# One transpose per score step, PV in fours, and the FFN 22 steps behind, in a fused attention and FFN kernel

## The chip, the cores and the metric

The kernel runs on one core of a Trainium2 chip. The metric is the device time of one execution in microseconds (us), the median of several runs. Engines are named as the profile names them: PE is the matrix engine (PEld its weight loads), DVE the vector engine, ACT the scalar engine, POOL the GpSimd engine, SP the engine whose queue issues most of the DMAs.

## The reference

Four batches of eight heads, 768 positions, head size 64. Queries and keys are each assigned to one of 16 clusters, and a query sees only the keys of its own cluster. The heads' outputs, side by side, are the 512 wide input of a gated FFN with 1536 hidden columns.

```python
q_assign = argmax(einsum('bhsd,hcd->bhsc', q_n, c_n), -1)   # k_assign the same way
mask = q_assign[:, :, :, None] == k_assign[:, :, None, :]
attn = softmax(where(mask, q @ k.T / sqrt(D), -1e9))
x = (attn @ v).transpose(0, 2, 1, 3).reshape(B * S, H * D)   # 3072 x 512
xn = x / sqrt(mean(x * x) + 1e-6) * rms_g
out = (silu(xn @ w_gate) * (xn @ w_val)) @ w_out             # 3072 x 512, float32
```

## The kernel before

The order of all instructions is written out by hand; each engine takes its own in that order, and a tile's next writer waits for its last readers.

**Steps and slots.** A *slot* is one head of one batch: 32 slots. The scores of a slot, keys on partitions, are 6 x 768 = 4608 columns, cut into nine *steps* of 512: 288 steps. In a step the loop calls `score_chunk`, then one piece of the FFN (`ffn_next`), then `flush(1)` (which lets all but the newest pending DVE operation go), then the product with v of the slot before (PV), then `extras`, the side work entered for that step with `at`.

**Scores.** Up to step `FFN0` two steps are taken together: up to four matmuls (L280) fill a 1024 column tile `scw` of which there are two, and one ACT exponential (L283) writes `pT`. A slot is so four wide chunks and a short one. From `FFN0` on each step has its own 512 column tile `sc`. The mask is 16 extra rows of `aug`: one-hot rows of the clusters, so the matmul has 80 rows.

**PV.** 36 matmuls of 65 columns a slot (L294), six a step in steps 2 to 7 of the next slot, into one accumulator `acc`; at its step 8 DVE takes the reciprocal of the sums and writes `x` (L303, L304).

**Preparation of a pair of heads** (`prep_parts`): twelve float32 transposes of q and k on PE in four groups of three (L183, T0 to T3), each group copied to `qk32` by DVE or ACT (L187, L189); casts to `aug` on POOL (L206); four cluster matmuls into `sp` (L222); on DVE the arg max (`tr`, `mx`, `oh`, `ohT`); four small DMAs on SP that place the one-hot rows in `aug`; the cast of v on POOL (L211). The tiles `tp` and `sp` share two buffers. Pair `pi` of 16 is used from step 18 `pi` on, and its parts lie at fixed steps after `base`, which is 18 (`pi` - 2) plus a small offset for pairs 2, 3 and 6.

**FFN.** A batch is two halves of 384 tokens, twelve blocks each of 128 hidden columns, and a block has three pieces: `gp` (four matmuls with the gate weights, ACT tanh `th`, then DVE `uu`), `vp` (four matmuls, then DVE `gvT`), and `dp` (three matmuls with the output weights, for the half before). `gp` and `vp` share two buffers (`gv`): a `gp` needs that the `uu` of the block before has read its buffer, a `vp` the `gvT` of the block before. After four `dp` pieces the sum goes through `ob` (DVE, or ACT in the tail) to the output; `dp` has one buffer. One piece is issued a step from `FFN0` = 72 + `LAG` on, with `LAG` = 24.

**Between them**, `rms_parts`: at step 8 of a batch's following slot its `x` is whole; in the steps after it the sums of squares `jk` (ACT, DVE), the power -0.5 on POOL (`ir`), three `xn` on DVE (L336), and one transposing DMA from SP to `xnT`, which the FFN reads; then the same for the second half. These lie at steps 9 to 26 after the batch's 72 steps.

**The tail** after step 287 issues what is left of the FFN. PSUM has eight banks: `ps_d` 1, `ps_pv` 1, `ps_t` 2, and four for `ps_wide`, given to `sc` and `gv` at `FFN0`.

Of the kernel before, what the change touches and what calls it, by code (L numbers as in the profile page):

```python
# [8 lines left out]
F32 = mybir.dt.float32  # L9
# [10 lines left out]
def kernel(  # L20
# [40 lines left out]
    ffn = ctx.enter_context(tc.tile_pool(name="ffn", bufs=2))  # L61
    ps_d = ctx.enter_context(tc.tile_pool(name="ps_d", bufs=1, space=PSUM))
    ps_pv = ctx.enter_context(tc.tile_pool(name="ps_pv", bufs=1, space=PSUM))
    ps_t = ctx.enter_context(tc.tile_pool(name="ps_t", bufs=2, space=PSUM))

    wide = ExitStack()
    ps_wide = wide.enter_context(tc.tile_pool(name="ps_wide", bufs=2, space=PSUM))
    late = {}
    LAG = 24
    FFN0 = H * NCH + LAG  # L70

# [48 lines left out]
    def keep_warm(n):  # L120
        w_ps = ps_d.tile([P, 512], F32, name="w_ps", tag="d")
        for _ in range(n):
            nc.tensor.matmul(w_ps, lhsT=zeros[:, 0:P], rhs=zeros, start=True, stop=True)
# [44 lines left out]
    def prep_parts(pi):  # L168
# [3 lines left out]

        def t_group(g):
            a, side = divmod(g, 2)
            if g == 0:
                qk32[0] = prep.tile([P, 4, HS], F32, name="qk32", tag="qk32")
            if pi == 0 and g >= 2:
                tp = ps_wide.tile([P, 2 * CH], F32, name="tpw", tag="scw")[:, 0:HS]
            else:
                tp = ps_t.tile([P, HS], F32, name="tp", tag="t")  # L180
            src = loads[pi][side]
            for i in range(TH):
                nc.tensor.transpose(tp[:, i * P:(i + 1) * P], src[:, a, i * P:(i + 1) * P], ident_f)  # L183
            dst = qk32[0][:, g, :]
            on_dve = (g % 2 == 0 if pi == 0 else g > 1 if pi == 1 else pi < 6 or g % 2)
            if on_dve:
                nc.vector.tensor_copy(dst, tp)  # L187
            else:
                nc.scalar.copy(dst, tp)  # L189
            state[g] = tp  # L190

# [21 lines left out]

        def assign():
            h0 = 2 * (pi % NP)
            if pi == 0:
                sp = ps_d.tile([P, CH], F32, name="spd", tag="d")[:, 0:HS]
            else:
                sp = ps_t.tile([P, HS], F32, name="sp", tag="t")
            for j in range(4):  # L220
                side, a = divmod(j, 2)
                nc.tensor.matmul(sp[32 * j:32 * j + 32, :], lhsT=cbd[:, h0 + a, :, :].rearrange("p c r -> p (c r)"),  # L222
                                 rhs=qk32[0][:, 2 * a + side, :], start=True, stop=True,
                                 tile_position=(0, 32 * j))
            state["sp"] = sp

# [28 lines left out]

        return [lambda: t_group(0), lambda: t_group(1), lambda: t_group(2), lambda: t_group(3), casts, assign, argmax1, argmax2, place, casts_v]

# [28 lines left out]

    def pv_group(slot, g):
        pi, a = divmod(slot, 2)
        vb = vbf[pi % NSET]
        if g == 0:  # L290
            accs[slot] = ps_pv.tile([P, ST, D + 1], F32, name="acc", tag="acc")
        acc = accs[slot]
        for kc in range(ST):
            nc.tensor.matmul(acc[:, TORD[g], :], lhsT=pts[slot][:, kc * S + g * P:kc * S + (g + 1) * P],  # L294
                             rhs=vb[:, a, TORD[kc], :], start=(kc == 0), stop=(kc == ST - 1))

    def pv_norm(slot):
# [55 lines left out]

    def ffn_piece(n, kind, tail):
        half = n // FC
# [26 lines left out]
        elif kind == 2 and half >= 1:  # L382
            hf = half - 1
            b, m = divmod(hf, 2)
            t = m * TH + fc // 4
            qd = fc % 4
            if qd == 0:
                pool, tag = (ps_pv, "acc") if tail and (fc // 4) % 2 else (ps_d, "d")
                cur["d"] = pool.tile([P, DM], F32, name="dp", tag=tag)
            dp = cur["d"]  # L390
            for i in range(3):
                f = qd * 3 + i
                tl = fc // 4
                nc.tensor.matmul(dp, lhsT=gvT[hf][:, f, tl * P:(tl + 1) * P], rhs=wo[:, f, :],  # L394
                                 start=(f == 0), stop=(f == FC - 1))
            if qd == 3:
                def after():
                    ob = ffn.tile([P, DM], F32, name="ob", tag="ob", bufs=3)
                    if tail:
                        nc.scalar.activation(ob, dp, ACT.Copy, scale=0.5)  # L400
                    else:
                        nc.vector.tensor_scalar_mul(ob, dp, 0.5)  # L402
                    nc.sync.dma_start(out=out_v[b, :, t, :], in_=ob)
                pend.append(after)
# [7 lines left out]

    def ffn_next(limit, tail=False):
        n, kind = divmod(fpos[0], 3)
        if n >= limit:
            return False
        fpos[0] += 1
        ffn_piece(n, kind, tail)
        return True
# [8 lines left out]

    T0, T1, T2, T3, CAST, SP, ARG1, ARG2, PLACE, CASTV = range(10)
    p0, p1 = prep_parts(0), prep_parts(1)  # L430
    keep_warm(6)
    for i in (T0, T1, T2, T3):
        p0[i]()
# [5 lines left out]
    p0[ARG1]()  # L439
    p1[T0]()  # L440
    p0[ARG2]()
    p0[PLACE]()
    for i in (T1, T2, T3, CAST):
        p1[i]()
    keep_warm(8)
    for i in (SP, ARG1, ARG2, PLACE, CASTV):
        p1[i]()
    load_pair(3)
    at(4, lambda: load_pair(4))
    at(30, lambda: nc.sync.dma_start(out=g_b, in_=moe_rms_g.unsqueeze(0).to_broadcast([P, DM])))  # L450
    for pi in range(2, B * NP):
        base = 2 * NCH * (pi - 2) + {2: 4, 3: 1, 6: 6}.get(pi, 0)
        for fn, step in zip(prep_parts(pi), (0, 1, 3, 4, 5, 8, 9, 11, 11, 9)):
            at(base + step, fn)
        if pi < B * NP - 3:
            at({6: 100, 7: 106}.get(pi, base + 11), lambda pi=pi: load_pair(pi + 3))
    for i, step in enumerate((50, 58, 68, 76, 86, 94, 100, 105, 111, 117, 123, 129)):
# [10 lines left out]
    for step in range(NT):  # L468
        slot, j = divmod(step, NCH)
        if step == FFN0:  # L470
            wide.close()
            for nm in ("sc", "gv"):
                late[nm] = ctx.enter_context(tc.tile_pool(name="ps_" + nm, bufs=2, space=PSUM))
        score_chunk(slot, j)
        ffn_next(min(B, max(0, (step - LAG) // (H * NCH))) * 2 * FC)
        flush(1)
        if slot > 0 and 2 <= j < 2 + ST:
            pv_group(slot - 1, j - 2)
        if slot > 0 and j == 2 + ST:
            pv_norm(slot - 1)  # L480
        extras(step)

    for j in range(28):
# [4 lines left out]
        flush(1)  # L488
        if 2 <= j < 2 + ST:
            pv_group(NS - 1, j - 2)  # L490
        if j == 2 + ST:
            pv_norm(NS - 1)
        extras(NT + j)
# [32 lines left out]
```

## Time and profile before

| | |
|---|---|
| median of 3 runs | 366.11 us (364.82 to 366.2) |
| the profiled execution | 365.05 us, its span 363.2 us |
| mean granted PE clock | 0.989 |
| PE busy | 335.2 us, 92% of the span |
| ACT / DVE / POOL busy | 229.4 / 223.5 / 86.3 us |
| PE's share of the chain that ended last | 72% (DVE 14%, ACT 7%) |
| first exponential of the scores, first FFN matmul, last exponential (start) | 15.9, 76.0, 282.8 us |

The profile is of one execution, 1.06 us below the median, and 1.8 us of its time lie outside the span. Its 40 slices are 9.08 us each. So the kernel has four stages: until 15.9 us the first loads and the preparation of two pairs; then ten slots of scores and PV alone, until the FFN begins at 76.0 us; then scores, PV and FFN together until 283 us; then the tail.

### The profile page before, as it was taken

What the parts mean: (1) busy time and instruction counts of PE and PEld (TensorE: products, weight loads), DVE (VectorE), ACT (ScalarE), POOL (GpSimd) and SP (SyncE); (2) the same over time, 40 slices, a digit from 0 to 9 for tenths busy, and PEclk for the clock granted to TensorE, in tenths of its full rate; (3) what the DMA queues carried; (4) which work ended last, traced back from release to release, by engine and by line L of the source; (5) the groups of instructions that cost most, each with busy time, mean ns of one, the idle gap of its engine ahead of it and who ended that gap; (6) DMA issues with size and microseconds to landing.
All of it is one profiled execution on the core that took longest, in us unless ns stands there. A gap on an engine that the chain in (4) does not pass through costs nothing.

```text
span 363.2 us, 7436 instructions
## 1 busy us (share of the span) xinstructions
PE 335.2 (92%) x2896; PEld 202.7 (56%) x2930; DVE 223.5 (62%) x445; ACT 229.4 (63%) x414; POOL 86.3 (24%) x119
## 2 busy tenths in 40 slices
PE   7688988699999999999999999999999979999996
PEld 3345656355665655656565655656666635555542
DVE  5676563777666658685746659685554687655540
ACT  4488889847777768767676768767777333232321
POOL 2644660772604041411213041410000011000000
PEclk9999999969999999999999999999999999999999
DMA  7449599289991402534050103131000022100012
GB/s 255 149 126 310 157 223 218 51 105 192 257 229 42 164 10 53 163 80 163 0 170 32 33 11 54 31 81 36 29 2 31 31 54 71 50 31 29 31 58 87
DMA packets 38242, 35.38 MB, mean 97 GB/s; under 512 B 15072, under 2 KB 35008, under 8 KB 38208
## 3 DMA queue, kind: packets, MB, share of 16 engines
q1 hardware_dynamic: 32080, 30.06, 26.9%
q0 software_dynamic: 5888, 4.77, 9.4%
q8 instruction: 23, 0.38, 0.4%
q10 hardware_dynamic: 240, 0.08, 0.1%
q14 instruction: 11, 0.09, 0.1%
HBM read 28.61 MB, written 6.29 MB: 96 GB/s over the span
## 4 chain that ended last, share of the span: by engine, by line
PE 72%; DVE 14%; ACT 7%; issue 3%; DMA 2%; POOL 2%; ACTq 0%; POOLq 0%; SPq 0%; DVEq 0%
PE vp L365 15%; PE gp L365 15%; PE dp L394 15%; PE sc L280 10%; PE acc L294 7%; PE tp L183 5%; ACT pT L283 4%; DVE xn L336 3%; PE scw L280 3%; PE sp L222 2%; ACT jk L319 1%; DVE gvT L380 1%; DVE oh L237 1%; DVE ohT L242 1%; DMA k_in<-in_k_dram 1%
## 5 line engine op out<-in xcount | busy, mean ns | idle before, releaser
L283 ACT ACTIVATE pT<-sc 128x512 bf16<-128x512 f32 x192 | 113.4, 598 | 55.4 <-PE sc L280 54.2
L374 DVE SCALAR_TENSOR_TENSOR uu<-th,gp 128x384 f32<-128x384 f32 x96 | 53.1, 553 | 72.4 <-ACT th L370 71.9
L365 PE MATMUL vp<-xnT,wv 128*128 128x384 bf16 x384 | 78.6, 327 | 2.1 <-DVE gvT L380 1.9
L365 PE MATMUL gp<-xnT,wg 128*128 128x384 bf16 x384 | 78.8, 327 | 0.4 <-DVE uu L374 0.3
L370 ACT ACTIVATE th<-gp 128x384 f32<-128x384 f32 x96 | 47.2, 492 | 49.9 <-PE gp L365 47.0
L394 PE MATMUL dp<-wo,gvT 128*128 128x512 bf16 x255 | 71.0, 378 | 5.9 <-DVE ob L402 3.1
L206 POOL CAST aug<-qk 64x768 bf16<-64x768 f32 x60 | 51.9, 865 | 101.2 <-DVE qk L187 98.3
L280 PE MATMUL sc<-aug 80*128 80x512 bf16 (+1 forms) x256 | 73.4, 328 | 0.0
L294 PEld LDWEIGHTS <-pT 128*128 128x128 bf16 x1152 | 58.2, 98 | 26.5 <-DVE x L304 0.8
L294 PE MATMUL acc<-vbf,pT 128*128 128x65 bf16 x1152 | 63.3, 194 | 0.5 <-DVE x L304 0.3
L380 DVE TENSOR_TENSOR gvT<-uu,vp 128x384 bf16<-128x384 f32 x96 | 52.6, 548 | 6.5 <-PE vp L365 1.4
L365 PEld LDWEIGHTS <-wg 128*128 128x128 bf16 x384 | 37.4, 98 | 29.9 <-issue 2.1
L283 ACT ACTIVATE pT<-scw 128x1024 bf16<-128x1024 f32 (+1 forms) x53 | 47.2, 946 | 9.6 <-PE scw L280 9.0
L365 PEld LDWEIGHTS <-wv 128*128 128x128 bf16 x384 | 37.2, 97 | 22.0 <-issue 3.8
L280 PEld LDWEIGHTS <-aug 80*128 80x128 bf16 x384 | 34.1, 98 | 27.4 <-issue 11.6
L394 PEld LDWEIGHTS <-gvT 128*128 128x128 bf16 x288 | 27.9, 97 | 30.3 <-issue 5.5
L280 PE MATMUL scw<-aug 80*128 80x512 bf16 (+1 forms) x128 | 29.2, 329 | 7.2 <-ACT pT L283 6.3
L187 DVE COPY qk<-tp 128x384 f32<-128x384 f32 x39 | 21.4, 554 | 23.2 <-PE tp L183 23.2
L327 POOL TENSOR_SCALAR ir<-ss 128x3 f32<-128x3 f32 x8 | 1.6, 195 | 99.7 <-ACT jk L319 97.6
L336 DVE SCALAR_TENSOR_TENSOR xn<-x,ir,g_b 128x512 bf16<-128x512 bf16 x24 | 20.7, 871 | 4.2 <-POOL ir L328 4.1
L183 PE MATMUL tp<-ident_f,k_in 128*128 128x128 f32 x93 | 16.3, 285 | 4.2 <-DVE qk L187 1.7
L304 DVE TENSOR_TENSOR x<-acc,inv 128x384 bf16<-128x384 f32 x32 | 17.8, 557 | 1.1
(64 smaller groups left out, 200.2 us busy)
## 6 DMA issues: line engine op xcount, KB each, us to landing
q_in<-in_q_dram SPq DMA_DIRECT2D x16, 384.0 KB, 4.4
k_in<-in_k_dram SPq DMA_DIRECT2D x16, 384.0 KB, 4.9
v_in<-in_v_dram SPq DMA_DIRECT2D x16, 384.0 KB, 5.6
out_dram<-ob SPq DMA_DIRECT2D x24, 256.0 KB, 2.0
wg<-in_moe_w_gate_dram POOLq DMA_DIRECT2D x4, 384.0 KB, 6.8
wv<-in_moe_w_val_dram POOLq DMA_DIRECT2D x4, 384.0 KB, 7.5
wo<-in_moe_w_out_dram POOLq DMA_DIRECT2D x4, 384.0 KB, 7.1
aug<-ohT SPq DMA_DIRECT2D x60, 24.0 KB, 2.8
```

What stands on the lines that cost most here:

```text
L183: nc.tensor.transpose(tp[:, i * P:(i + 1) * P], src[:, a, i * P:(i + 1) * P], ident_f)
L187: nc.vector.tensor_copy(dst, tp)
L206: nc.gpsimd.tensor_copy(aug[st][a][0:D, :, par * HS:(par + 1) * HS], qk32[0][par * D:(par + 1) * D, 2 * a:2 * a + 2, :])
L280: nc.tensor.matmul(sc[:, o:o + n], lhsT=ag[:, 1, kc * P:(kc + 1) * P], rhs=ag[:, 0, qo:qo + n], start=True, stop=True)
L283: nc.scalar.activation(pts[slot][:, j * CH:(j + nch) * CH], sc[:, :nch * CH], ACT.Exp, scale=scale)
L294: nc.tensor.matmul(acc[:, TORD[g], :], lhsT=pts[slot][:, kc * S + g * P:kc * S + (g + 1) * P], rhs=vb[:, a, TORD[kc], :], start=(kc == 0), ...
L336: nc.vector.scalar_tensor_tensor(st["xn"][:, tl, :], x_t[b][:, t, :], st["ir"][:, tl:tl + 1], g_b, op0=ALU.mult, op1=ALU.mult)
L365: nc.tensor.matmul(pt[:, :HS], lhsT=w[:, dc, fc * P:(fc + 1) * P], rhs=xnT[b, m][:, :, dc, :], start=(dc == 0), stop=(dc == DC - 1))
L370: nc.scalar.activation(th, pt[:, :HS], ACT.Tanh, scale=0.5)
L374: nc.vector.scalar_tensor_tensor(uu, th, 1.0, pt[:, :HS], op0=ALU.add, op1=ALU.mult)
L380: nc.vector.tensor_tensor(gvT[half][:, fc, :], uu, pt[:, :HS], op=ALU.mult)
L394: nc.tensor.matmul(dp, lhsT=gvT[hf][:, f, tl * P:(tl + 1) * P], rhs=wo[:, f, :], start=(f == 0), stop=(f == FC - 1))
```

## The change

- **Transposes.** `t_group` becomes `t_one`: one transpose a step at `base` + 0 to 11, the copy after every third. The casts move from `base` + 5 to + 12, the cluster matmuls from + 8 to + 13 and + 14 (two halves of 192 columns each, `SPA` and `SPB`), the first part of the arg max from + 9 to + 15, its second part and the placing DMAs from + 11 to + 17, the cast of v from + 9 to + 14, the load of pair `pi` + 3 from + 11 to + 17. The offset of pair 6 becomes 5.
- **PV.** For slots 0 to 8 (`NFAST` = 9) four matmuls in every step 0 to 8, the accumulators taken by turns from `ps_pv` and a new one-bank pool `ps_pv2`. Later slots keep six a step. `ps_pv2` takes the bank of `ps_d`, and `dp` gets its bank at `FFN0`.
- **FFN.** `LAG` is 22: the first piece is at step 94, and each batch's FFN begins two steps earlier against its scores.
- **`ob`.** It goes to ACT in steps 8 to 27 of each 72 and in the whole of what follows step 287, and to DVE otherwise.

```diff
-    ps_d = ctx.enter_context(tc.tile_pool(name="ps_d", bufs=1, space=PSUM))
...
+    ps_pv2 = wide.enter_context(tc.tile_pool(name="ps_pv2", bufs=1, space=PSUM))
     late = {}
-    LAG = 24
+    LAG = 22
     FFN0 = H * NCH + LAG
...
-        def t_group(g):
+        def t_one(n):
+            g, i = divmod(n, TH)
             a, side = divmod(g, 2)
...
-            for i in range(TH):
-                nc.tensor.transpose(tp[:, i * P:(i + 1) * P], src[:, a, i * P:(i + 1) * P], ident_f)
+            nc.tensor.transpose(tp[:, i * P:(i + 1) * P], src[:, a, i * P:(i + 1) * P], ident_f)
+            if i < TH - 1:
+                return
             dst = qk32[0][:, g, :]
...
-        def assign():
+        def assign(cols=slice(0, HS)):
...
-                nc.tensor.matmul(sp[32 * j:32 * j + 32, :], lhsT=cbd[:, h0 + a, :, :].rearrange("p c r -> p (c r)"),
-                                 rhs=qk32[0][:, 2 * a + side, :], start=True, stop=True,
+                nc.tensor.matmul(sp[32 * j:32 * j + 32, cols],
+                                 lhsT=cbd[:, h0 + a, :, :].rearrange("p c r -> p (c r)"),
+                                 rhs=qk32[0][:, 2 * a + side, cols], start=True, stop=True,
                                  tile_position=(0, 32 * j))
...
+    NFAST = FFN0 // NCH - 1
+    def pv_some(slot, n0, n1):
...
+            pool = ps_pv2 if slot < NFAST and (NFAST - slot) % 2 else ps_pv
+            accs[slot] = pool.tile([P, ST, D + 1], F32, name="acc", tag="acc")
...
+    def pv_step(slot, j):
+        if slot < NFAST:
+            pv_some(slot, 4 * j, 4 * j + 4)
+        elif 2 <= j < 2 + ST:
+            pv_some(slot, (j - 2) * ST, (j - 1) * ST)
+        if j == 2 + ST:
+            pv_norm(slot)
...
-                    if tail:
+                    if on_act:
                         nc.scalar.activation(ob, dp, ACT.Copy, scale=0.5)
...
-    at(4, lambda: load_pair(4))
+    at(6, lambda: load_pair(4))
...
-        base = 2 * NCH * (pi - 2) + {2: 4, 3: 1, 6: 6}.get(pi, 0)
-        for fn, step in zip(prep_parts(pi), (0, 1, 3, 4, 5, 8, 9, 11, 11, 9)):
+        base = 2 * NCH * (pi - 2) + {2: 4, 3: 1, 6: 5}.get(pi, 0)
+        for fn, step in zip(prep_parts(pi), (*range(NTR), 12, 13, 14, 15, 17, 17, 14)):
             at(base + step, fn)
         if pi < B * NP - 3:
-            at({6: 100, 7: 106}.get(pi, base + 11), lambda pi=pi: load_pair(pi + 3))
+            at({6: 100, 7: 108}.get(pi, base + 17), lambda pi=pi: load_pair(pi + 3))
...
-        ffn_next(min(B, max(0, (step - LAG) // (H * NCH))) * 2 * FC)
+        ffn_next(min(B, max(0, (step - LAG) // (H * NCH))) * 2 * FC,
+                 on_act=8 <= step % (H * NCH) < 28)
         flush(1)
-        if slot > 0 and 2 <= j < 2 + ST:
-            pv_group(slot - 1, j - 2)
-        if slot > 0 and j == 2 + ST:
-            pv_norm(slot - 1)
+        if slot > 0:
+            pv_step(slot - 1, j)
         extras(step)
```

## The prediction

> **What bounds the kernel now.** I read the busy shares by stage first, then the waits, then the timeline around the places that the change touches. The stages (columns: stretch, its length, busy us of PE, PEld, DVE, ACT, POOL, then PE clock, DMA share, GB/s):
>
> ```profile
> 15.86:61.96 46.10, 39.31 (x485) 26.49 (x484) 27.82 (x58) 39.97 (x47) 21.63 (x27) 1.00 0.76 191
> 61.96:76.02 14.06, 9.78 (x105) 6.36 (x102) 10.35 (x19) 11.00 (x19) 8.71 (x11) 0.87 0.51 102
> 76.02:283.00 206.98, 202.62 (x1833) 125.72 (x1858) 133.38 (x268) 148.81 (x288) 47.74 (x60) 0.99 0.33 84
> 283.00:363.20 80.20, 72.41 (x419) 39.01 (x424) 43.21 (x82) 23.47 (x50) 2.09 (x4) 1.00 0.15 50
> ```
>
> In the score stage (row 1) ACT is ahead: 40.0 of 46.1 us. In the hand-over (row 2) no engine is full and the clock sinks. In the long FFN stage (row 3) PE is busy 202.6 of 207.0: anything added to PE there is paid in full. Now the waits (us in all, times, longest):
>
> ```profile
> ACT pT L283 <- PE scw L280: 9.0, 16, 2.3
> PE dp L394 <- DVE ob L402: 3.1, 3, 1.7
> PE vp L365 <- DVE gvT L380: 1.9, 4, 0.8
> ```
>
> ACT waits 9.0 us for wide scores. PE loses 3.1 us in three places, one at each later batch boundary, to an `ob` that DVE holds behind `xn`. These are what the change aims at. The timeline shows what its parts cost (start, length, engine, line, operation):
>
> ```profile
> 66.02 3.75 DVE L336 SCALAR_TENSOR_TENSOR xn<-x,ir,g_b 128x512 bf16<-128x512 bf16 x3 [2.54 <-POOL ir L328]
> 65.95 4.51 POOL L206 CAST aug<-qk 64x768 bf16<-64x768 f32 x4
> 69.80 1.38 SPq L339 DMA_TRANSPOSE xnT<-xn  x1
> 126.38 0.49 PE L183 MATMUL tp<-ident_f,k_in 128*128 128x128 f32 x3
> 126.70 0.38 PE L280 MATMUL sc<-aug 80*128 80x512 bf16 x1
> 128.81 0.52 PE L183 MATMUL tp<-ident_f,q_in 128*128 128x128 f32 x3
> 129.17 0.38 PE L280 MATMUL sc<-aug 80*128 80x256 bf16 x2
> 134.18 0.59 PE L394 MATMUL dp<-wo,gvT 128*128 128x512 bf16 x2
> 134.70 0.85 PE L222 MATMUL sp<-qk,cbd 128*32 128x384 f32 x8
> 135.49 0.39 PE L280 MATMUL sc<-aug 80*128 80x512 bf16 x1
> 140.08 0.75 DVE L336 SCALAR_TENSOR_TENSOR xn<-x,ir,g_b 128x512 bf16<-128x512 bf16 x1 [0.16 <-POOL ir L328]
> 140.75 0.69 DVE L402 TENSOR_SCALAR ob<-dp 128x512 f32<-128x512 f32 x1
> 141.49 0.81 PE L394 MATMUL dp<-wo,gvT 128*128 128x512 bf16 x2 [0.71 <-DVE ob L402]
> ```
>
> To see: three `xn` beside POOL's casts take 3.75 us, one without a cast 0.75. Three transposes after an FFN piece take 0.33 us until the next score (126.38 to 126.70), after PV 0.36 (128.81 to 129.17): after the short PV matmuls the first transpose costs 0.03 more. And `sp` makes PE wait.
>
> **Score stage, steps 0 to 80: -0.75 us.** A wide exponential follows the last in 0.904 us; from the start of the last wide one to the next slot's first takes another 1.99 (its 0.904 and 1.084 for the short chunk with the wait behind it). The slot from 42.48 to 47.20 has no preparation and takes 4.72; those from 37.15 and 47.20, with four groups of transposes, take 5.33. The new order does not shorten the first kind: its 0.46 us ACT wait hangs on the score buffer, not on PV. Of the second kind, a pair of steps costs PE 0.43 (scores) + 8 x 0.03 (PV) + 2 x 0.14 (single transposes after PV) = 0.95, against ACT's 0.90 and some 0.05 of slack: about 0.02 a pair, 4.8 a slot. But `sp`, in two halves, now lies inside a slot; before, it lay for pairs 4 and 5 at the slot's end, under ACT's short chunk, and cost nothing. Half an `sp` is 0.56 (next but one part). One in a pair of steps gives 0.43 + 0.24 + 0.56 = 1.23, 0.28 late; both in one pair, as for pairs 4 and 5, 0.83 late. Slots 0 to 8: 4.7, 4.8, 5.25, 5.05, 4.8, 5.55, 4.8, 5.55, 4.85 = 45.35 us. Step 81 starts at 61.2 instead of 61.96. From both sides: nothing gained, or 1.8 (all slots but those with `sp` at 4.72).
>
> **Hand-over, steps 81 to 100: -3 us more.** From step 81 (61.2) ACT has the exponential (0.9), two `jk` (0.77, 0.7): 63.6. From the end of the second `jk` to `xn` the trace of before has 1.3 us: 64.9. The casts that slowed `xn` before now come after (step 89), so three at 0.745: 67.15 instead of 69.7. The transposing DMA landed 3.7 to 6.0 us after issue in its eight cases; with weights under way I take 5.3: 72.4, against 75.7 before, and the first `gp` follows at once, at step 94 instead of 96. DVE no longer stops PE at a transpose (1.7 us at 70.3). PE still stands some 2 us before 72.4, so I let the clock fall again. It was at half from 72.3 to 79.1 (6.83 us); now PE has work without a gap from 72.4 on, and I take half that stretch, until 75.7; the ends are no fall at all and 79.1 again. The Trainium skill ("TensorE: Matmul & The Clock Gate", Part 1) states activity windows of 3413 ns, of which 6.83 us is two, and that one busy window frees the clock: by the page 75.7 and the sum below, by the whole stretch of the row a sum 1.7 us higher. Counting on at half speed to 75.7, `vp` of block 1 (step 98) starts at 77.9 and step 100 at 79.1; before, step 100 had its `vp` of block 1 at 81.6. That is 2.5 us, 0.65 for the `vp` already done, and 0.6 for half of the two `gvT` waits of before (0.77 at 85.1, 0.46 at 101.9): 3.7 together with the score stage. From both sides: 0, if the DMA takes 6 us and the clock stays low until 79.1; 5.3, if the clock holds.
>
> **Single transposes in the FFN stage: +1.4 us.** Pairs 7 to 15. Before, two of the twelve transposes came first after PV; now seven do (those in a slot's steps 2 to 7 and in step 2 of the next): 5 x 0.032 x 9. At least 0 (the load fits under PV), at most 3.5 (each single one as dear as 0.03 over the mean of 0.11).
>
> **`sp` in halves: +2.2 us.** The last `dp` before `sp` starts at 134.39 by the trace and lasts 0.215, so `sp` could start at 134.61; it starts at 134.70, its second pass at 135.05, the next score at 135.49: 0.09 wait, 0.35, 0.44 of which 0.1 is draining: 0.88. A half then is 0.09 + 0.19 + 0.28 = 0.56, two 1.12, so 0.24 more, in nine pairs. From below 0.5 (only the drain doubles in part), from above 4 (a pass does not shrink with its columns).
>
> **Batch boundaries at some 140 and 222 us: +4.2 us.** Two things meet. First, with `LAG` 22 other pieces lie under the `rms` steps: `ob` now comes before `xn` and on ACT, so its 0.71 (0.68) us stall goes. But DVE's order becomes `uu`, `xn`, `xn`, `gvT`, `xn`, and the second `vp` after that needs this `gvT` for its buffer. Second, POOL's casts of pairs 10 and 14, before at step 5 of the batch's slot, are now at step 12, right behind `ir`, beside the three `xn`. Count from the start of step 152: scores 0.22, FFN 0.65, PV 0.19, transposes 0.11 to 0.14 put that `vp` (step 158, with one half `sp` before it) at 7.0. ACT reaches the second `jk`'s end at 5.25 (copy 0.36, two exponentials 0.55, `th` 0.45, `ob` 0.57, two `jk` 0.77, after `x` at 1.0 and PE's pace), `xn` at 6.6, two of them at 1.3: 9.2, `gvT` 0.55: 9.75. PE stands 2.8 us, 2.1 more than now, twice. What is queued behind the waiting `xn` on DVE is `gvT` and `uu`; who waits is PE. With `xn` at 0.745, as it is here now without casts, it is 1.7, 1.0 more. The three at 66.0, beside casts, took 1.30 each, and I take that row. The Trainium skill ("SBUF — State Buffer", Who interferes with whom) says that a DVE operation with two SBUF inputs and a GpSimd one that reads SBUF exclude each other for a whole instruction; the rows at 66.0 agree, the rule speaks against this change, and by it the sum is the one below, by the lone 0.745 it would be 2.2 lower. Bounds: -1.4 (both stalls simply go) to +5.
>
> **Tail: +0.8 us.** Here no casts run. `ob` on ACT comes between the two `jk`, so `xn` is 0.6 later than its 3.6 us after `x`; `dp` waits 0.6 for `ob`, `vp` 2.65 for `gvT`: 3.25 instead of 2.4 (1.75 + 0.32 + 0.32). Bounds -1.75 to +1.5.
>
> **At nothing:** the second accumulator (same bank count, its readers long done), the later loads and placing DMAs (SP has nothing urgent behind them; pair 2's rows land about when slot 4 starts, 35.7 us: if 1 us late, 1 us lost), the other `ob` copies (ACT is idle 58 of 207 us there).
>
> **Sum.** -3.7 + 1.4 + 2.2 + 4.2 + 0.8 = +4.9 on the profiled execution's 365.05: 370.0. The median lies 1.06 above that execution; with half of it, 370.5. A measurement of this kernel can tell about 0.5%, 1.8 us, from no change.
>
> **Rivals.**
> - *`ob` was the whole stall* (faster). At the three boundaries DVE keeps up once `ob` is on ACT: the 3.1 us of that wait go and none comes: -3.7 + 3.6 - 3.1 = -3.2, some 362. For: the wait is named in the profile, and nothing else holds PE there now. Against: the three `xn` stay in DVE's order ahead of `gvT`, and `xn` waits for `ir`. It decides from the point at which the boundaries give back more than 1.7 us. Chance 0.18, range 360 to 364.2.
> - *The boundaries stay as they are*: -3.7 + 3.6 = about 365 to 366.5. Chance 0.13.
> - *The hand-over gives nothing*: the DMA is late and the clock stays at half. Then + 8.6 instead of 4.9: 374. For: 5.9 us of landing before, and PE again stands before the DMA. Chance 0.14.
> - *My forecast*: 0.55, own range 367.9 to 373.
>
> The range 364 to 374.5 leaves out most of the fastest rival and the end of the slowest, under 2 in 10. Faster 0.18, same 0.13, slower 0.69.
>
> **What would show it.** Right: quiet slots still 4.7 us apart in ACT's exponentials, transposing ones near 4.8, a slot with both halves of `sp` near 5.5; `xn` near 67 done; first `gp` at 71 to 73; each pair's two `sp` 1.1 us in all in the FFN stage; `PE vp <- DVE gvT` over 5 us in the waits with `PE dp <- DVE ob` gone; `xn` at 1.3 at the two middle boundaries. Wrong: `gvT` waits under 2 us, the first `gp` after 75, or PE's FFN stage no longer per step than now.

## The result and the profile after

The changed kernel takes 379.98 us (median of 4 runs, 379.1 to 382.52), against 365.6 for the one before (4 runs, 364.82 to 366.2): a ratio of 1.0406, 95% interval 1.0347 to 1.0465. That is 14.4 us slower. The forecast was 4.9 us slower, with a range that ended at 374.5: the direction was right, the size was not. A run more than 1.5% above the fastest of its kernel counts as slow, and is left out of the ratios here and below but not out of the medians and ranges.

The profiled execution took 379.23 us, its span 377.5. The stages of its profile, as the prediction showed them for before (stretch, its length, busy us of PE, PEld, DVE, ACT, POOL, then PE clock, DMA share, GB/s):

```profile
17.36:62.57 45.21, 40.72 (x517) 28.38 (x516) 26.92 (x58) 39.82 (x46) 19.91 (x25) 1.00 0.69 179
62.57:74.90 12.33, 9.19 (x91) 5.47 (x89) 8.99 (x16) 9.39 (x17) 8.25 (x10) 0.86 0.87 180
74.90:297.37 222.47, 209.84 (x1934) 132.46 (x1959) 132.75 (x266) 153.72 (x297) 49.84 (x61) 0.99 0.32 78
297.37:377.50 80.13, 71.42 (x413) 38.35 (x418) 41.44 (x78) 24.02 (x52) 2.09 (x4) 1.00 0.15 50
```

Only row 3 is bad. Before, PE stood idle there for 4.4 us (206.98 less 202.62); now it stands idle for 12.6. The stage also has two more FFN pieces in it, because the FFN starts two steps earlier, so I compare steps from here on. Times are the starts of ACT's exponentials in the two profiled executions:

| stretch | before | after | difference | forecast |
|---|---|---|---|---|
| span's start to step 0 | 15.9 | 17.4 | +1.5 | 0 |
| steps 0 to 81 (score stage) | 46.1 | 45.2 | -0.9 | -0.75 |
| steps 81 to 99 (hand-over) | 19.0 | 17.8 | -1.2 | -3, of which -1.75 up to step 100 |
| steps 99 to 279 (FFN stage) | 193.8 | 208.9 | +15.2 | +7.8 |
| step 279 to the end (tail) | 88.5 | 88.1 | -0.4 | +0.8 |

The waits (us in all, times, longest) name what PE now stands for:

```profile
PE vp L385 <- DVE gvT L400: 13.7, 15, 2.3
...
PE dp L414 <- ACT ob L420: 1.9, 4, 0.7
```

The 3.1 us for DVE's `ob` are gone, as forecast, and `gvT` stands in their place. But 13.7 us in 15 waits is more than the batch boundaries can hold. Nine of the fifteen are not at boundaries at all: they come once for each of pairs 7 to 15, and they sum to 7.26 us (0.99, 0.99, 0.75, 1.08, 0.47, 0.47, 0.74, 1.08, 0.69). The timeline shows one (DVE, then PE; the bracket is the idle time before):

```profile
173.44 0.56 DVE L394 SCALAR_TENSOR_TENSOR uu<-th,gp 128x384 f32<-128x384 f32 x1 [0.75 <-ACT th L390]
173.91 0.19 DVE L323 RECIPROCAL inv<-acc 128x6 f32<-128x6 f32 x1
174.14 0.56 DVE L324 TENSOR_TENSOR x<-acc,inv 128x384 bf16<-128x384 f32 x1
174.61 0.58 DVE L242 TENSOR_TENSOR oh<-tr,mx 128x384 bf16<-128x384 f32 x1
175.22 0.25 DVE L244 TENSOR_SCALAR oh<-oh 64x384 bf16<-64x384 bf16 x1
175.51 0.58 DVE L247 STREAM_TRANSPOSE ohT<-oh 128x384 bf16<-128x384 bf16 x1
176.01 0.52 DVE L400 TENSOR_TENSOR gvT<-uu,vp 128x384 bf16<-128x384 f32 x1
```

```profile
176.58 0.81 PE L385 MATMUL vp<-xnT,wv 128*128 128x384 bf16 x4 [0.47 <-DVE gvT L400]
```

Between `uu` and `gvT` DVE does five other things: the norm of PV (`inv`, `x`) and the second part of the arg max (`oh`, `oh`, `ohT`). They fill it from 173.91 to 176.01. The next `vp` needs the buffer that this `gvT` reads, and PE stands 0.47 us, in other pairs up to 1.08.

The profile of before already had this in small, where the arg max alone comes between `uu` and `gvT`. Pair 7 (DVE, then PE):

```profile
82.52 0.55 DVE L374 SCALAR_TENSOR_TENSOR uu<-th,gp 128x384 f32<-128x384 f32 x1
82.98 0.58 DVE L237 TENSOR_TENSOR oh<-tr,mx 128x384 bf16<-128x384 f32 x1
83.60 0.40 DVE L239 TENSOR_SCALAR oh<-oh 64x384 bf16<-64x384 bf16 x1
84.03 0.58 DVE L242 STREAM_TRANSPOSE ohT<-oh 128x384 bf16<-128x384 bf16 x1
84.53 0.52 DVE L380 TENSOR_TENSOR gvT<-uu,vp 128x384 bf16<-128x384 f32 x1
```

```profile
85.10 0.65 PE L365 MATMUL vp<-xnT,wv 128*128 128x384 bf16 x3 [0.77 <-DVE gvT L380]
```

The wait of 0.46 us at 101.9 us, for pair 8, stands behind the same order. The norm lies elsewhere there. In six of the nine pairs of before the arg max alone stands between `uu` and `gvT`; the four after these two cost 0.11 us at most.

### The profile page after: what moved, and what is told of

The parts are those of the page before. It is cut to its first block, busy times and chain, and to the rows that moved or that the text cites. A ratio compares the mean times of both kernels' runs of the same rounds, so it can differ in the third digit from the quotient of the medians.

```text
span 377.5 us, 7654 instructions
## 1 busy us (share of the span) xinstructions
PE 344.5 (91%) x3007; PEld 210.7 (56%) x3042; DVE 218.8 (58%) x439; ACT 233.1 (62%) x421; POOL 87.7 (23%) x119
## 4 chain that ended last, share of the span: by engine, by line
PE 70%; DVE 14%; ACT 10%; issue 3%; POOL 1%; DMA 1%; SPq 0%; ACTq 0%; DVEq 0%
PE vp L385 14%; PE dp L414 14%; PE gp L385 13%; PE sc L287 9%; PE acc L306 7%; ACT pT L290 5%; PE tp L185 4%; PE sp L227 4%; PE scw L287 4%; DVE xn L356 3%; ACT th L390 2%; DVE uu L394 2%; DVE gvT L400 2%; DVE x L324 2%; DVE oh L242 2%
## 5 line engine op out<-in xcount | busy, mean ns | idle before, releaser
L385 PE MATMUL vp<-xnT,wv 128*128 128x384 bf16 x384 | 78.6, 327 | 13.7 <-DVE gvT L400 13.7
L306 PEld LDWEIGHTS <-pT 128*128 128x128 bf16 x1152 | 63.7, 99 | 29.0 <-issue 2.3
L209 POOL CAST aug<-qk 64x768 bf16<-64x768 f32 x60 | 53.7, 895 | 104.7 <-DVE qk L191 101.2
L287 PE MATMUL sc<-aug 80*128 80x256 bf16 (+1 forms) x259 | 74.2, 328 | 0.0
L414 PE MATMUL dp<-wo,gvT 128*128 128x512 bf16 x254 | 69.4, 379 | 3.8 <-ACT ob L420 1.9
L306 PE MATMUL acc<-vbf,pT 128*128 128x65 bf16 x1152 | 70.0, 194 | 0.2
L290 ACT ACTIVATE pT<-scw 128x1024 bf16<-128x1024 f32 (+1 forms) x52 | 46.1, 944 | 12.2 <-PE scw L287 12.1
L287 PEld LDWEIGHTS <-aug 80*128 80x128 bf16 x384 | 37.7, 105 | 23.9 <-issue 12.4
L185 PE MATMUL tp<-ident_f,q_in 128*128 128x128 f32 x93 | 26.6, 303 | 1.3 <-ACT qk L193 0.9
L185 PE MATMUL tp<-ident_f,k_in 128*128 128x128 f32 x93 | 26.6, 302 | 1.0 <-DVE qk L191 0.8
```

Source lines behind the costliest of these rows:

```text
L209: nc.gpsimd.tensor_copy(aug[st][a][0:D, :, par * HS:(par + 1) * HS], qk32[0][par * D:(par + 1) * D, 2 * a:2 * a + 2, :])
L287: nc.tensor.matmul(sc[:, o:o + n], lhsT=ag[:, 1, kc * P:(kc + 1) * P], rhs=ag[:, 0, qo:qo + n], start=True, stop=True)
L290: nc.scalar.activation(pts[slot][:, j * CH:(j + nch) * CH], sc[:, :nch * CH], ACT.Exp, scale=scale)
L385: nc.tensor.matmul(pt[:, :HS], lhsT=w[:, dc, fc * P:(fc + 1) * P], rhs=xnT[b, m][:, :, dc, :], start=(dc == 0), stop=(dc == DC - 1))
```

## The experiments

All times are medians in us; each ratio is against the kernel before, run on the same chip (its medians there were 364.9 to 366.2). In the diffs `STEPS` stands for the tuple `(*range(NTR), 12, 13, 14, 15, 17, 17, 14)`.

### Which part costs: one part undone at a time

**The second part of the arg max three steps later** (`arg2_later`, pairs 7 to 15), and the placing DMAs with it:

```diff
+        a2 = 20 if pi > 6 else 17
-        ... zip(prep_parts(pi), (*range(NTR), 12, 13, 14, 15, 17, 17, 14)):
+        ... zip(prep_parts(pi), (*range(NTR), 12, 13, 14, 15, a2, a2, 14)):
```

> After, but for pairs 7 to 15 the second part of the arg max and the placing DMAs lie at base + 20 instead of + 17, so no longer in the step in which DVE also normalises a slot. Theory 'DVE order' (the waits of the second FFN block half for gvT, 13.7 us in the changed kernel's trace, come from DVE work that meets in one step): the nine once-a-pair waits of 0.47 to 1.08 us (7.2 us in sum) go, 5 to 7 us faster than the changed kernel, some 374. Rival 'PE work' (the added cost is what single transposes and halved cluster matmuls take on PE, and the waits only show where PE happens to stand): within 1 us of 380. Rival 'FFN two steps earlier' (the new place of FFN pieces against the rms steps): within 1 us of 380.

Measured: 373.9 (372.36 to 378.69), ratio 1.0192 (1.0145 to 1.0238), as the first theory had it. The nine waits are gone (the profiled execution is the one of 378.69, with five stretches at half clock before its end; I read its waits, not its time); 6.4 us in 6 waits for `gvT` are left, 5.8 of them at the two middle boundaries (1.80 and 1.75) and in the tail (2.28).

**The cluster matmuls in one piece** (`sp_whole`) at +13, instead of two halves at +13 and +14:

```diff
+        parts = prep_parts(pi)
+        parts[SPA], parts[SPB] = parts[SP], lambda: None
-        for fn, step in zip(prep_parts(pi), STEPS):
+        for fn, step in zip(parts, STEPS):
```

> After, but the cluster matmuls are one group again (384 columns, at base + 13). 'PE work' by the rows of the changed kernel's trace: a half costs 0.56 us, a whole 0.88, so 0.24 us a pair in nine pairs of the FFN stage and up to 0.8 us a slot in two slots of the score stage: 2 to 3.5 us faster, 376.5 to 378. 'DVE order' expects the same here, and the gvT waits unchanged within 1 us of 13.7. If the halves were hidden: no difference.

Measured: 375.29 (374.11 to 377.39), ratio 1.025 (1.0201 to 1.0299), so 4.7 us less than the change, more than any theory said. Its FFN stage, steps 99 to 279, is 204.6 instead of 208.9. Of these 4.4 us, 0.64 are shorter stalls at the boundaries (1.47 and 1.43 instead of 1.79 and 1.75) and 1.7 a stretch at half clock that does not come (below); that leaves 2.1 for the halves themselves, where the prediction had 2.2.

**The FFN 24 steps behind again** (`lag_24`):

```diff
-    LAG = 22
+    LAG = 24
```

> After, but the FFN 24 steps behind as before. 'FFN two steps earlier': most of the loss goes, 8 to 12 us faster, 368 to 372. 'DVE order': only the two batch boundaries change (1.8 us each now, 0.7 before), partly given back at the hand-over (2 pieces later, about 0.7): 1 to 3 us faster, 377 to 379. 'PE work': no difference.

Measured: 374.55 (373.63 to 375.65), ratio 1.0225 (1.0184 to 1.0265), 5.4 less, between the two theories that expected a gain. The waits for `gvT` fall to 7.5 us in 8.

**The whole preparation as before** (`old_prep`), with the rest of the change:

```diff
+        parts = prep_parts(pi)
+        parts[SPA], parts[SPB] = parts[SP], lambda: None
-        for fn, step in zip(prep_parts(pi), STEPS):
+        for fn, step in zip(parts, (0, 0, 0, 1, 1, 1, 3, 3, 3, 4, 4, 4, 5, 8, 8, 9, 11, 11, 9)):
```

(the loads and the offset of pair 6 also as before)

> After, but the preparation of a pair as before: three transposes a step at base + 0, 1, 3, 4, casts + 5, one whole cluster matmul group + 8, arg max + 9 and + 11, loads + 11. What stays of the change: PV in fours with two accumulators, FFN 22 steps behind, ob on ACT. 'DVE order' and 'PE work' both expect most of the loss to go: 365 to 369, with gvT waits under 4 us. 'FFN two steps earlier': stays over 374.

Measured: 371.31 (370.55 to 373.6), ratio 1.0145 (1.0087 to 1.0203), between the two ranges expected. The FFN stage is 195.1, nearly that of before, but steps 81 to 99 take 21.7.

The single effects (6.1, 4.7, 5.4, 8.7) sum to 24.9, far more than the 14.4 us lost: the edits overlap, and the last contains the first two.

### One part at a time on the kernel before

**`ob` on ACT alone** (`ob_on_act`), in the steps in which the change puts it there:

```diff
-                    if tail:
+                    if on_act:
```

> Before, with only ob on ACT in steps 8 to 27 of each 72 and after step 287. The rival of the prediction ('ob was the whole stall'): the waits of 0.71, 0.68 and 1.75 us go and none comes, 3 us faster, 362 to 363. 'DVE order': the three xn still stand before uu and gvT, so a wait of 0.3 to 1.5 us for these takes the place of each: 0 to 2 us faster, 364 to 366.

Measured: 363.3 (362.08 to 364.3), ratio 0.9918 (0.9882 to 0.9953). The first rival of the prediction ("`ob` was the whole stall") names something real: on the old order this edit gives 2.3 us, between the two expectations. In the profiled executions 0.8 of it lie in the FFN stage (193.0) and 0.5 in the tail, where waits of 1.05 us for `uu` and 0.42 for `ob` on ACT take the place of the 1.75. The hand-over, in which no `ob` lies, is 1.7 shorter too, with one half clock stretch of 3.41 us instead of 6.83, so not all of the 2.3 need come from `ob`. At the two middle boundaries nothing over 0.16 us is left: it is the rest of the change that puts other waits there.

**The new preparation alone** (`prep_only`), that is the change with PV, `ob` and the FFN as before:

```diff
-    LAG = 22
+    LAG = 24
-    NFAST = FFN0 // NCH - 1
+    NFAST = 0
-                 on_act=8 <= step % (H * NCH) < 28)
+                 on_act=False)
...
-            ffn_next(2 * FC * (B - 1))
+            ffn_next(2 * FC * (B - 1), on_act=False)
```

> Only the new preparation (single transposes, halved cluster matmuls, later steps); FFN 24 steps behind, PV six a step into one accumulator, ob on DVE as before. 'DVE order' and 'PE work' together: nine pairs at 0.40 us of PE work (3.6 us), the arg max beside the slot's normalisation (about 3.5 us of gvT waits with 24 steps, by the trace of the kernel with the FFN 24 steps behind), casts beside xn at two boundaries (some 1.3 us), 1 to 2 us back in the score stage and hand-over: 372 to 375. If the new preparation were harmless by itself: 364 to 368.

Measured: 374.36 (372.22 to 376.03), ratio 1.021 (1.0161 to 1.026). The new order of the preparation alone costs 8.7 us, as expected.

### The parts put together

**The arg max at +20 and the cluster matmuls in one piece** (`arg2_sp_whole`, the edits of `arg2_later` and `sp_whole` in one):

> After, with both: second part of the arg max at base + 20 for pairs 7 to 15, cluster matmuls whole. If the two causes add: 6 + 4 us less than 380, 369.5 to 371.5, and in the trace gvT waits only at the hand-over, the two boundaries and the tail. If they are the same time counted twice (PE standing in one place or the other): 372 to 375.

Measured: 367.34 (364.54 to 370.1), ratio 1.003 (0.9996 to 1.0064). 12.6 of the 14.4 us are back with these two edits, more than the 10 expected of their sum. 5.5 us in 5 waits for `gvT` are left.

**The same with the FFN 24 steps behind** (`arg2_sp_lag24`, `LAG = 24` in addition):

> The change with all three suspects undone: second part of the arg max at +20 for pairs 7 to 15, the cluster matmuls in one piece, the FFN 24 steps behind. If the suspects add up: 367.3 less what the two steps cost, 363 to 365, with what is left of the loss in the single transposes (1.4 us) and the casts beside xn. If the two steps cost only through the first two: 367, +-1.

Measured: 363.07 (360.61 to 365.0), ratio 0.9949 (0.9915 to 0.9983), as expected of the sum, now 1.5 us in 5 waits for `gvT`. So the loss has three main causes: the place of the arg max, the halves, and the two steps.

**A hybrid** (`hybrid`): the new steps for pairs 2 to 5 alone, whose steps lie in the score stage; the rest prepared as before; the cluster matmuls of all pairs in one piece; 24 steps behind; PV in fours and `ob` as in the change:

```diff
+        parts = prep_parts(pi)
+        parts[SPA], parts[SPB] = parts[SP], lambda: None
+        if pi < 6:
+            steps = (*range(NTR), 12, 13, 14, 15, 17, 17, 14)
+        else:
+            steps = (0, 0, 0, 1, 1, 1, 3, 3, 3, 4, 4, 4, 5, 8, 8, 9, 11, 11, 9)
```

> The parts that should help, where they should help: single transposes at the new steps only for pairs 2 to 5 (score stage) with the cluster matmuls whole, pairs 6 to 15 prepared as before, PV in fours with two accumulators, ob on ACT, FFN 24 steps behind. 'DVE order': score stage 0.9 us shorter as in the changed kernel's trace, no gvT waits once a pair, batch boundaries under 0.7 us each, so 1 to 4 us faster than before: 362 to 365. 'PE work': 0 to 1 us faster. If it is slower than before, PV in fours or ob on ACT costs something that no row has shown.

Measured: 361.86 (360.68 to 363.91), ratio 0.9876 (0.9837 to 0.9914): the lowest ratio of all, and faster than before. Steps 0 to 81 take 44.7. Against `arg2_sp_lag24` (0.9949) only the preparation of pairs 6 to 15 differs (and their loads): its single transposes and later steps are left as a cost of 1.2 us by the medians, 2.7 by the ratios, which no run takes apart.

**The hybrid with the FFN 22 steps behind** (`hybrid_lag22`, `LAG = 22`):

> The hybrid (score steps rewritten for pairs 2 to 5 alone, the preparations of pairs 6 to 15 as in the kernel before) with the FFN 22 steps behind, as in the change, in place of 24. Theory A, the two steps are harmless by themselves and cost only beside the rewritten steps: 362, +-1, the hand-over from the score steps to the FFN 2 us shorter and the tail the same. Theory B, the earlier FFN costs by itself, since its first step comes at 81, while xn for it is still to be transposed by DMA: as in the run with the preparation of before and the FFN 22 steps behind (371.3, steps 81 to 99 in 21.7 us, one wait of 1.87 us for xnT, 10.2 us at half clock) 366 to 370, with a wait of over 1 us for gvT at both boundaries.

Measured: 370.31 (368.39 to 371.29), ratio 1.0139 (1.0102 to 1.0176). PE's waits in the two hybrids (first 24, then 22 steps behind):

```profile
PE vp L385 <- DVE gvT L400: 2.4, 5, 0.9
```

```profile
PE vp L385 <- DVE gvT L400: 6.8, 9, 2.3
...
PE gp L385 <- DMA xnT<-xn: 2.3, 1, 2.3
```

So theory B holds: the two steps cost 8.4 us by themselves. Between the profiled executions it is 7.1, of which 4.3 lie in the hand-over (steps 81 to 99 take 21.7 instead of 17.4): the first FFN step now comes before `xnT` has landed, PE stands 2.3 us, and a stretch at half clock falls on FFN work at 77.4 to 80.8 (with 24 steps there were as many us at half clock, 67.9 to 74.7, but they ended before the FFN began). 2.3 lie in the FFN stage: stalls of 1.29 and 1.26 us at the boundaries, where there was one of 0.16.

**The hybrid with PV in sixes** (`hybrid_pv_six`, `NFAST = 0`):

> The hybrid with PV of all heads at six matmuls a step into one accumulator, as before. If PV in fours is worth nothing where the steps are bound by TensorE's sum of work: 362, +-0.7. If the even spread of PV in the score steps of pairs 2 to 5 is what the hybrid gains by: up to 1.5 more, 363 to 363.5, all of it before step 99.

Measured: 362.35 (361.82 to 362.56), ratio 0.9924 (0.9894 to 0.9954). The interval overlaps that of the hybrid: PV in fours is worth no more than these runs can tell (the score stage of the profiled execution is 0.5 us longer without it).

### What exactly of the arg max costs

I had put the nine waits down to the norm and the arg max in the same step. That was tested first with the arg max one step later (`arg2_next_step`: `sp_whole` with `a2 = 18` in place of 17 for pairs 7 to 15):

> The change with the cluster matmuls in one piece and the second part of the arg max one step later, +18, in place of +20 (367.3). If it is that VectorE has the norm of PV and the arg max in the same step: 367, +-1, no once-a-pair wait for gvT. If it is that VectorE is late anywhere near the steps without PV, the wait only moves: 369 to 373, with waits of 0.3 to 1 us for gvT once a pair.

Measured: 376.18 (375.2 to 377.27), ratio 1.0306 (1.0264 to 1.0349), which fits neither: nothing was gained over +17 (375.29). DVE's timeline shows why:

```profile
108.57 0.56 DVE L324 TENSOR_TENSOR x<-acc,inv 128x384 bf16<-128x384 f32 x1
109.04 0.58 DVE L242 TENSOR_TENSOR oh<-tr,mx 128x384 bf16<-128x384 f32 x1
...
110.44 0.51 DVE L400 TENSOR_TENSOR gvT<-uu,vp 128x384 bf16<-128x384 f32 x1
```

The order is the same as at +17. `flush(1)` holds the newest pending DVE operation back, and lets it go only when a newer one comes. With the FFN 22 steps behind, the pieces of a slot are `gp` in steps 1, 4 and 7, `vp` in 2, 5 and 8, `dp` in 0, 3 and 6. The `gvT` of step 8 is pending while the norm is issued; step 0 is a `dp` piece and mostly adds nothing pending; so this `gvT` is issued in step 1. What is entered at +17 (step 8) or at +18 (step 0) comes ahead of it, what is entered at +19 behind it. Two runs test this reading, both with the halves and everything else of the change. One moves the arg max to +19 (`arg2_plus19`, the edit of `arg2_later` with `a2 = 19`):

> The change, with only the second part of the arg max of pairs 7 to 15 moved from +17 to +19. Order theory: what costs is the place in VectorE's order. A step lets all but the newest pending operation go, so gvT of the vp in step 8 of a slot is issued only in step 1 of the next; at +17 and at +18 the arg max (1.4 us) comes between the norm of PV (0.75 us) and this gvT, at +19 behind it. Then the nine waits of 0.47 to 1.1 us once a pair (7.2 us in all) go at +19 as they did at +20: 373 to 374.5. Rival, VectorE has too much to do around the steps without PV (8, 0 and 1): +19 is one of them, the waits stay in part, 376 to 379.

Measured: 375.01 (372.53 to 376.88), ratio 1.0269 (1.0209 to 1.0328). The nine waits are gone (6.4 us in 6 left). The time is half a microsecond above what was expected; the profiled execution has a half clock stretch behind both middle boundaries and one in the tail, which by half their length cost 1.7 us each. The other (`gvt_first`) leaves the arg max where it is and issues `gvT` first:

```diff
-        flush(1)
+        flush(0 if j == 8 and slot % 2 else 1)
```

> The change, with one line more: in step 8 of every second slot (where the second part of the arg max lies at +17) nothing is kept pending, so gvT of that step's vp comes in VectorE's order ahead of the norm and the arg max, which stay in the same step. Order theory: the nine once-a-pair waits go, 7.2 us less than the change, 373 to 374.5, although not one instruction has moved to another step but gvT. Rival, too much for VectorE around the steps without PV: 2.2 us of norm and arg max then stand before the next uu and gvT instead, waits for these of the same size, 377 to 380.

Measured: 373.31 (371.71 to 375.18), ratio 1.0243 (1.0182 to 1.0305). Its DVE and PE in a place like the one above:

```profile
169.57 0.55 DVE L400 TENSOR_TENSOR gvT<-uu,vp 128x384 bf16<-128x384 f32 x1
170.04 0.19 DVE L323 RECIPROCAL inv<-acc 128x6 f32<-128x6 f32 x1
...
171.65 0.58 DVE L247 STREAM_TRANSPOSE ohT<-oh 128x384 bf16<-128x384 bf16 x1
```

```profile
171.42 0.81 PE L385 MATMUL vp<-xnT,wv 128*128 128x384 bf16 x4
```

The same work in the same step, in another order, and the next `vp` starts without a wait; all nine waits are gone. One line gives back 6.7 us. It is DVE's order, not its load: what costs is the norm and the arg max together ahead of one `gvT`. The arg max alone stands there in all nine pairs of `arg2_sp_lag24`, and no wait there is longer than 0.25 us.

### The boundaries

One run asked what the casts beside `xn` cost: `gvt_first`, with the transposes and casts of pairs 10 and 14 alone as before, so that POOL is done with the casts before `xn`.

```diff
+        tc12 = (0, 0, 0, 1, 1, 1, 3, 3, 3, 4, 4, 4, 5) if pi in (10, 14) else (*range(NTR), 12)
-        for fn, step in zip(prep_parts(pi), STEPS):
+        for fn, step in zip(prep_parts(pi), (*tc12, 13, 14, 15, 17, 17, 14)):
```

> As gvt_first (373.3), and for pairs 10 and 14 alone, which are prepared beside the rms steps of a batch, the transposes and casts as in the kernel before: four groups of three at +0, +1, +3 and +4, casts at +5, so that POOL has them done before ir and the three xn. Theory A, the forecast's boundary term: xn beside the casts (1.26 to 1.31 each) is what makes PE stand 1.79 and 1.75 us at the two middle boundaries: xn 0.75 to 0.85 each, the stalls 0.6 to 1.0 us, 1 us less each, and no half clock stretch behind them (1.7 us where there is one), 369.5 to 371.5. Rival B, it is the order uu, xn, xn, gvT that comes with the FFN 22 steps behind, and xn starts when ir is there whatever POOL does after: stalls of 1.6 to 1.8, 373, +-1.

Measured: 370.1 (367.12 to 372.86), ratio 1.008 (1.0049 to 1.0112), against 373.31 and 1.0243 without: 3.2 us less by the medians, some 6 by the ratios (the two ran on different chips, so the ratios are the fairer measure). The boundary in the change (DVE, PE, POOL):

```profile
143.03 2.53 DVE L356 SCALAR_TENSOR_TENSOR xn<-x,ir,g_b 128x512 bf16<-128x512 bf16 x2 [1.11 <-POOL ir L348]
145.48 0.54 DVE L400 TENSOR_TENSOR gvT<-uu,vp 128x384 bf16<-128x384 f32 x1
...
146.08 1.40 PE L385 MATMUL vp<-xnT,wv 128*128 128x384 bf16 x4 [1.79 <-DVE gvT L400]
...
142.97 4.51 POOL L209 CAST aug<-qk 64x768 bf16<-64x768 f32 x4
```

and in `casts_early`:

```profile
141.15 1.96 DVE L356 SCALAR_TENSOR_TENSOR xn<-x,ir,g_b 128x512 bf16<-128x512 bf16 x2 [1.85 <-POOL ir L348]
143.03 0.54 DVE L400 TENSOR_TENSOR gvT<-uu,vp 128x384 bf16<-128x384 f32 x1
```

Two `xn` take 1.96 us instead of 2.53. The first still lies beside a cast, that of v, and takes 1.30; the second takes 0.74. The stalls fall from 1.79 and 1.75 to 1.28 and 1.24: 0.5 each, not the 1 us expected. In the profiled executions the FFN stage falls from 200.4 to 198.0: these 1.0 us, and a half clock stretch that does not follow. So the casts are part of the stalls; 1.2 us of each stay with the order `uu`, `xn`, `xn`, `gvT`, and `hybrid_lag22`, which has that order and its casts as before, shows the same (1.29 and 1.26). That the transposes of these two pairs go back into groups, 0.3 us by the prediction's unit, was not separated.

## Why the prediction went wrong, point by point

**The step that failed is a term that is not there.** The arg max's second part, 1.4 us of DVE, went from `base` + 11 to + 17, and no term of the prediction prices that. "At nothing" lists the accumulator, the loads, the placing DMAs and the `ob` copies; the arg max went in at zero without a reason, and where it lands in DVE's order is nowhere asked. It lands behind the norm and ahead of a `gvT` that PE's next `vp` needs; before, it stood ahead of a `gvT` as well in six of the nine pairs, but without the norm. Its price is 7.26 us by the nine waits, 6.7 by `gvt_first`, 6.1 by `arg2_later`. With it, the forecast of 370.5 would have been about 377.8. The prediction had two smaller waits of this kind in hand, 0.77 at 85.1 and 0.46 at 101.9, and counted half of them as a gain without asking what stood in front of that `gvT`. Its sign of being right, "`gvT` over 5 us", came true, but more than half of the 13.7 us for this reason that it did not have.

**Start: not forecast, and not of the change.** The 1.5 us before step 0 are a stretch at half clock, 13.03 to 16.45 us, that the profiled execution of before did not have. PE did the same two pieces of work there (after, then before):

```profile
12.48 2.65 PE L123 MATMUL w_ps<-zeros 128*128 128x512 bf16 x7
15.49 1.29 PE L227 MATMUL sp<-qk,cbd 128*32 128x384 f32 x8 [0.36 <-issue]
```

```profile
12.61 1.67 PE L123 MATMUL w_ps<-zeros 128*128 128x512 bf16 x7
14.43 0.85 PE L222 MATMUL sp<-qk,cbd 128*32 128x384 f32 x8
```

Other runs with this same first stage began their first exponential at 16.0 (full clock from 4.7 us on) to 21.1 us (full clock only from 12.3 on, and a stretch at half clock after it).

**Score stage: right.** -0.9 measured, -0.75 forecast; 45.2 us for steps 0 to 81 against 45.35. The two slots that held both halves of `sp` took 5.53 and 5.62 (forecast 5.55), as the working had it.

**Hand-over: the size right, but by steps that were wrong.** Counted as the prediction counted, from step 81 to step 100, it is 18.3 us instead of 20.0, so -1.7, where -1.75 was forecast. The other 1.25 of the -3 lie behind that: the two `gvT` waits of before went whole (-1.2, in the FFN stage of the table), and the `vp` already done belongs to the tail, which has two pieces less. But the first `gp` came 12.3 us after step 81, not 11.2 (at 74.9, forecast 72.4). What failed here is that the casts would come after `xn`. In the timeline (DVE, POOL, SP, PE) they do not:

```profile
66.26 3.80 DVE L356 SCALAR_TENSOR_TENSOR xn<-x,ir,g_b 128x512 bf16<-128x512 bf16 x3 [2.59 <-POOL ir L348]
...
67.02 2.50 POOL L209 CAST aug<-qk 64x768 bf16<-64x768 f32 x2
...
70.09 1.38 SPq L359 DMA_TRANSPOSE xnT<-xn  x1
...
74.89 0.81 PE L385 MATMUL gp<-xnT,wg 128*128 128x384 bf16 x4
```

POOL does not wait for the step in which an instruction was entered. It took the two casts whose rows were already copied as soon as it was free, and the three `xn` took 1.27 each instead of 0.745, 1.6 us in all. `xn` began 3.7 us after step 81, as forecast; the 66.26 instead of 64.9 is the later start. The transposing DMA landed after 4.1 us (5.3 assumed), at 74.19, and the half clock stretch was one of 3.41 us (71.06 to 74.47), which is the half of 6.83 that I took, but it was over before the first `gp`. These two made up for the casts: that is luck.

**Single transposes: right in the unit.** One behind PV keeps PE 137 to 145 ns (median 140) until the next score matmul, against 109 behind other work: 0.031 each (0.032 taken), 1.4 us.

**`sp` in halves: right in the unit, too small in effect.** A half took 0.56 us (0.10 more than the usual spacing after the last PV matmul, then 0.19 and 0.28 for its two passes). Undone, it gives 4.7 us, because without the halves each boundary stall is 0.32 us shorter as well and, in the profiled execution, no half clock stretch follows them.

**Boundaries: the mechanism right, the size too large, and one thing left out.** The `ob` stalls of 0.71 and 0.68 went and `gvT` stalls of 1.79 and 1.75 came: +2.15 instead of +4.2. Counted from the start of step 152, the two `xn` began at 6.0 us (forecast 6.6) and `vp` could have begun at 7.3 (forecast 7.0), so PE stood 1.8 us and not 2.8. The first two `xn` beside the casts took 1.28 to 1.31, as in the rows at 66.0. The Trainium skill ("SBUF — State Buffer", Who interferes with whom) says that a DVE instruction with two SBUF inputs contends with a GpSimd instruction that reads SBUF; the runs agree: the third `xn`, which starts in the last 0.3 us of a cast, took 0.84, and those beside none took 0.74. What was left out is the 1.7 us of half clock behind the stall at 146.1 us.

**Tail:** -0.4 instead of +0.8. The forecast stalls came (2.28 and 0.27 for `gvT` around 312 us; PE's waits there sum to 4.7 us instead of 3.8, so +0.9), but what is left of the FFN in the tail is two steps shorter, which the term did not count.

**FFN stage in sum:** 7.26 (arg max) + 2.15 (boundaries) + 1.7 (half clock) + 1.4 (transposes) + 2.2 (halves) - 1.2 (the two `gvT` waits of before at 85 and 102 us) = 13.5 of the 15.2 us. `gvt_first` shows where most of the rest lies: with one half clock stretch in this stage, as in the change, it takes 200.4 instead of 208.9, 8.6 less. PE's idle time falls by 7.3 (12.6 to 5.3), its busy time by 1.3 (196.4 to 195.1). So the order cost 8.6 rather than 7.26, and 0.4 stay untraced. A sum with 8.6 ends at 379.1, close to the 379.98 measured, but only because the start (+1.5) and the half clock (+1.7) offset the boundaries (2.0 below their forecast) and the tail (1.2 below).

**The two steps of `LAG`.** The prediction counted them as a gain in the hand-over and a loss at the boundaries and in the tail. `hybrid_lag22` shows a loss of 8.4 us on the old preparation, `arg2_sp_lag24` of 4.3 on the new one. Why `xnT` landed at 74.2 in the change but at 76.4 in `hybrid_lag22`, with `xn` done at 70.1 in both, is open. In `hybrid_lag22` POOL had all four casts to do first and issued a weight load at 70.7, beside the transposing DMA; in the change it issued that load at 66.2. But in `sp_whole` the load went out at 65.4, and its transposing DMA still took 5.5 us, against 4.1 in the change.

## What to carry to other kernels

When a change moves an operation on a shared engine, write down that engine's order around its new place and ask which operation behind it releases a buffer of the engine that sets the time; a step number says nothing about that where operations are held back. A mean load of 58% on DVE does not clear an edit: 1.4 us of arg max, put beside the norm and ahead of one `gvT`, nine times, cost more than all the PE time that was added. And entering an instruction later delays it only if something holds its engine until then.

## What the runs showed of the hardware

The granted clock changes on a fixed grid. Within each execution the stretches at half clock begin at multiples of 3.413 us from one another: in the changed kernel 13.03, 71.06 and 146.15 us, in `gvt_first` 71.09, 142.77 and 303.20. The changed kernel around the first middle boundary (columns as in the stages above):

```profile
142.60:146.08 3.48, 1.69 (x21) 0.79 (x20) 3.05 (x4) 1.79 (x4) 3.36 (x4) 1.00 0.03 13
146.15:149.56 3.41, 3.19 (x20) 1.47 (x21) 1.95 (x4) 0.38 (x1) 2.09 (x3) 0.50 0.48 92
```

A stall of 1.79 us that lies wholly in one window of this grid is here followed by a window at half clock, which costs some 1.7 us more (half of 3.41, PE being busy in nearly all of it). I laid the grid over the PE idle times of all seventeen profiled executions, leaving out windows that are at half clock themselves. In the FFN stage, six windows with 1.73 to 1.80 us idle were followed by half clock, and none with up to 1.68 was. The change's second boundary stall, 1.75 us, lay across two windows (1.52 in one), and nothing followed. So a stall of this length costs 1.7 us more or not by its place on the grid, which differs from run to run. The bound is not the same elsewhere, so idle time alone does not decide: in the hand-over windows with 1.42 us or more were followed by half clock and those with up to 1.38 were not, and in the tail four with 1.94 to 1.99 were not, while one with 1.85 and all with 2.15 or more were. What else counts, these runs do not show.

The Trainium skill ("TensorE: Matmul & The Clock Gate", Part 1) states that the window of 3413 ns is free-running, which the runs agree with. In the same part it gives as a rule that PE should have no idle gaps over some 3.4 us, and here 1.73 us was enough.
